# A gated recurrence and a long convolution on one core: h in time order with wrap copies, x1·x3 beside the spectral units, products summed by the inverse transform

## The chip, the cores and the metric

The kernel runs on one core of a Trainium2 chip. The core has a matrix engine (TensorE, PE in the profile, with its weight loads as PEld), a vector engine (VectorE, DVE), a scalar engine (ScalarE, ACT), a general engine (GpSimd, POOL), and a queue that here issues the transfers (SyncE, SP). Each works through its own list of instructions in order. The metric is device time in microseconds of one execution. All times below are microseconds unless ns is said.

## The reference

The inputs are x and f_logit of shape (4, 6272, 256): four batches (B), 6272 time steps (S), 256 channels (D). First comes a gated recurrence over time, then a projection into three parts, a circular convolution over the whole length by Fourier transform, a product of three, and an output projection:

```python
sig = 1.0 / (1.0 + np.exp(-f_logit))
f = lower_bound + (1.0 - lower_bound) * sig
for t in range(S):
    h = f[:, t] * h + (1.0 - f[:, t]) * x[:, t]
    y[:, t] = h
proj = y @ w_proj                          # 256 -> 3 x 256
x1, x2, x3 = proj[..., :D], proj[..., D:2*D], proj[..., 2*D:]
conv = irfft(rfft(x2, axis=1) * rfft(filter_fft, axis=0), n=S, axis=1)
out = (x1 * conv * x3) @ w_out
```

## The kernel before, in words

The transform of length 6272 is split into 128 × 49: with indices taken modulo S, a time step is addressed either as 49·m + r (natural order, m up to 128, r up to 49) or as 128·q + 49·m modulo S (rotated order, q up to 49). For each r there is one q (`Q_OF_R`), and the rows of one order are those of the other turned round by m0 (`m0_of`). So the transform is one of length 128 over m, followed by one of length 49 over q, with no twiddle factors between. `NEP` = 128 pairs of channels are worked in `NU` = 16 units of 8.

**hgrn(b)**, the recurrence, goes over 16 chunks of 392 time steps. Per chunk: x and f_logit are loaded (SP), the gate is a sigmoid on ACT, `xt` the product of x and gate on POOL (L123); 16 fp32 transposes on TensorE bring channels onto partitions (`sT`, `uT`); ACT makes `fT`, DVE runs the scan (L138), and POOL copies h out of natural order into `hG`, grouped by r (L143).

**prepare** builds the transform's matrices, the weights in high and low fp16 parts, and the filter's spectrum `H`: the filter is loaded in seven pieces (`fraw`), turned by 98 fp32 matmuls with a rotated identity (`pr`, L293), cast by ACT and DVE into `f2h` and `f2l` (L297, L298), and transformed in 16 units (`pfa`, `pfx`).

**phase_p(b)** copies h from `hG` into rotated order, `hP`, on POOL (L364, L366), multiplies by the x2 weights (`pp`) and evacuates on ACT (L370). **phase_f1(b)** does the 128-point transform, evacuated in turn by DVE (L386) and ACT (L388) into `A`. **phase_z(b)** computes x1·x3: eight 512-column matmuls with high and low weights (L406), x1 evacuated by ACT (`x1s`, L411), the product by DVE (L412). **mini(b)** does the frequency-0 column apart (`pm`, `zm`, L421). **units(b)**: per unit the 49-point transform (`px`, four matmuls, L442); the complex product with `H` as two wide multiplies (L446, L447) and two adds into `Y` (L450, L451) on DVE; POOL writes the frequency-0 column (L452); eight inverse matmuls (`pi`, L457, L459) with matrices `VA`, `VB`; ACT evacuates into `Th` (L463). **phase_o(b)**: the inverse over 128 (`pc`, L478), the product with x1·x3 on DVE (L482), the output projection (`po`, L491), ACT (L495), a store on SP.

The order is set in two ways. `weave` interleaves the loops of two phases by step count: recurrence of batch 0 with prepare; p, then f1, with x1·x3; units with the next batch's recurrence. Then a scheduler lists the instructions of each engine by that order as priority and by what is ready in its own reckoning, and the engines keep that list. PSUM tiles come from pools with one or two buffers: one for px (`psx`), two shared by all that is called `m` (`psm`), two for the transposes (`pst`).

## Time and profile before

| | |
|---|---|
| median of 3 runs | 1229.44 (1226.43 to 1230.41) |
| profiled execution | 1228.79, its span 1227.1 |
| mean granted TensorE clock | 0.803 of full speed |
| HBM | 58.85 MB read, 25.69 MB written |
| first x1·x3 matmul of batch 0, 1, 2, 3 | 242, 505, 765, 1015 |

The span runs from the first to the last instruction of the profiled execution. A busy share is an average over stages that have different limits, so the span is read stage by stage: preparation to 240, then four batches. The chain of waits is the work that ended last, followed back from the end; the timeline lists instructions by start. Matmuls overlap in the array, so four of them in a row take less than four times the length of one.

### The profile page before, as it was taken

To read this page: it belongs to the slowest core of one execution; us is meant where nothing else is said; L and a number is where in the kernel's file an instruction comes from. 1 tells how busy PE (TensorE), PEld (TensorE's weight loads), DVE (VectorE), ACT (ScalarE), POOL (GpSimd) and SP (SyncE) were. 2 spreads that over 40 slices of the span, in tenths; PEclk is the share of its full clock that TensorE was granted. 3 is DMA by queue.
4 is the path that set the end of the run, shared out by engine and by line. 5 is a ranking of instruction groups with operands and counts; after the bars stand their busy time and mean duration, and the time that the engine had idled before them with its cause. 6 is when DMAs were issued, how large, how long until landed. Compare 5 with 4: busy or idle time off the path is not lost.

```text
span 1227.1 us, 14846 instructions
## 1 busy us (share of the span) xinstructions
PE 892.4 (73%) x5784; PEld 577.3 (47%) x5784; DVE 639.7 (52%) x806; ACT 504.3 (41%) x649; POOL 386.8 (32%) x701
## 2 busy tenths in 40 slices
PE   2676789886678848776778677867788568767765
PEld 1444566443355536543455455434455454333344
DVE  7766743123579834223779632235898322346632
ACT  5676754463233324543333324633333226321122
POOL 5433441450136593000346761001465800000000
PEclk9996599999955569999755579998655799995579
DMA  6344411000023425100233334000233130000013
GB/s 199 97 124 122 122 56 51 28 1 1 2 78 105 114 78 190 65 1 1 53 82 111 97 123 168 1 1 26 68 106 91 52 141 19 1 1 0 1 69 142
DMA packets 61350, 85.50 MB, mean 70 GB/s; under 512 B 3040, under 2 KB 53984, under 8 KB 61280
## 3 DMA queue, kind: packets, MB, share of 16 engines
q1 hardware_dynamic: 61280, 84.55, 21.9%
q8 instruction: 45, 0.74, 0.3%
q14 instruction: 25, 0.20, 0.1%
HBM read 58.85 MB, written 25.69 MB: 69 GB/s over the span
## 4 chain that ended last, share of the span: by engine, by line
PE 46%; DVE 28%; POOL 9%; ACT 8%; issue 7%; DMA 3%; POOLq 0%; SPq 0%; DVEq 0%; ACTq 0%
PE p L406 15%; PE po L491 8%; PE px L442 5%; DVE z L482 4%; DVE p L446 4%; DVE z L412 4%; DVE Y L451 4%; ACT x1s L411 4%; PE pfx L324 3%; PE pr L293 3%; DVE A L386 3%; DVE h L138 3%; POOL hP L366 3%; POOL xt L123 3%; PE pc L478 2%
## 5 line engine op out<-in xcount | busy, mean ns | idle before, releaser
L143 POOL CAST hG<-h 128x392 f16<-128x392 f32 x128 | 109.6, 861 | 359.9 <-PE p L406 262.2
L406 PE MATMUL p<-hG,W13h 128*128 128x512 f16 (+1 forms) x416 | 150.3, 368 | 83.2 <-DVE z L412 42.5
L123 POOL TENSOR_TENSOR xt<-xt,ft 98x1024 f32<-98x1024 f32 x64 | 157.4, 2461 | 131.5 <-DMA xt<-in_x_dram 54.9
L412 DVE TENSOR_TENSOR z<-p,x1s 128x512 f16<-128x512 f32 (+1 forms) x104 | 68.4, 658 | 182.4 <-ACT x1s L411 182.4
L463 ACT CAST Th<-pi 128x784 f16<-128x784 f32 x64 | 52.0, 812 | 245.9 <-PE pi L459 245.9
L406 PE MATMUL p<-hG,W13l 128*128 128x512 f16 (+1 forms) x416 | 150.3, 367 | 0.0
L132 PE MATMUL uT<-iden,xt 98*128 98x98 f32 x512 | 107.2, 353 | 53.5 <-ACT fT L135 27.9
L482 DVE TENSOR_TENSOR z<-pc,z 128x1024 f16<-128x1024 f32 (+1 forms) x52 | 60.5, 1163 | 153.7 <-PE pc L478 153.7
L491 PE MATMUL po<-Woh,z 128*128 128x256 f16 x392 | 99.3, 294 | 55.1 <-DVE z L482 53.2
L442 PE MATMUL px<-A,FT 98*128 98x512 f16 x256 | 118.9, 593 | 27.0 <-DVE p L447 20.4
L411 ACT ACTIVATE x1s<-p 128x512 f32<-128x512 f32 (+1 forms) x104 | 59.5, 572 | 169.1 <-PE p L406 168.6
L138 DVE TENSOR_TENSOR_SCAN h<-fT,h,uT 128x392 f32<-128x392 f32 x120 | 120.6, 1024 | 11.2 <-PE uT L132 7.1
L132 PEld LDWEIGHTS uT<-iden,xt 98*128 98x128 f32 x512 | 80.0, 206 | 85.1 <-ACT fT L135 43.5
L128 PE MATMUL sT<-iden,ft 98*128 98x98 f32 x512 | 105.3, 352 | 19.4 <-ACT ft L122 16.0
L457 PE MATMUL pi<-VA,Y 98*128 98x196 f16 x256 | 84.4, 364 | 43.9 <-POOL Y L452 43.9
L491 PEld LDWEIGHTS <-z 128*128 128x128 f16 x784 | 77.9, 105 | 77.1 <-DVE z L482 62.2
L446 DVE TENSOR_TENSOR p<-px,H 98x1024 f16<-98x1024 f32 x64 | 78.2, 1222 | 64.0 <-PE px L442 64.0
L128 PEld LDWEIGHTS sT<-iden,ft 98*128 98x128 f32 x512 | 83.2, 210 | 45.2 <-issue 14.9
L495 ACT ACTIVATE osb<-po 128x1024 f32<-128x1024 f32 (+1 forms) x52 | 50.6, 974 | 129.0 <-PE po L491 122.4
L406 PEld LDWEIGHTS <-W13l 128*128 128x128 f16 x416 | 40.5, 97 | 131.5 <-issue 97.1
L135 ACT ACTIVATE fT<-sT,nomc 128x392 f32<-128x392 f32 x128 | 77.4, 605 | 53.7 <-PE sT L128 51.4
L491 PE MATMUL po<-Wol,z 128*128 128x256 f16 x392 | 98.6, 292 | 0.0
(129 smaller groups left out, 1522.4 us busy)
## 6 DMA issues: line engine op xcount, KB each, us to landing
xt<-in_x_dram SPq DMA_DIRECT2D x64, 392.0 KB
ft<-in_f_logit_dram SPq DMA_DIRECT2D x64, 392.0 KB
out_dram<-osb SPq DMA_DIRECT2D x48, 512.0 KB
fraw<-in_moe_filter_fft_dram SPq DMA_DIRECT2D x7, 896.0 KB
...
wcol<-in_lower_bound_dram SPq DMA_DIRECT2D x1, 1.0 KB
```

The costliest lines, as they stand in the source:

```text
L123: nc.gpsimd.tensor_tensor(xt[:TB], xt[:TB], ft[:TB], op=AOP.mult)
L128: nc.tensor.transpose(sT[:, j * TB:(j + 1) * TB], ft[:TB, j, cols], iden[:TB, :TB])
L132: nc.tensor.transpose(uT[:, j * TB:(j + 1) * TB], xt[:TB, j, cols], iden[:TB, :TB])
L138: nc.vector.tensor_tensor_scan(h32[:], fT[:], uT[:, 0:CH], 0.0 if last[kh] is None else last[kh][:, CH - 1:CH], op0=AOP.mult, op1=AOP.add)
L143: nc.gpsimd.tensor_copy(hG[b][:, kh, :, c * MR:(c + 1) * MR], h32[:].rearrange("p (m r) -> p r m", r=Q))
L406: nc.tensor.matmul(p13[:, i, 0:cn], w[:, kh, js], hG[b][:, kh, r0:r0 + rn, :], start=(n == 0), stop=(n == 3))
L411: nc.scalar.activation(x1s[:, 0:cn], p13[:, 0, 0:cn], AF.Copy, scale=ZS)
L412: nc.vector.tensor_tensor(z[:, jb, r0:r0 + rn, :], p13[:, 1, 0:cn], x1s[:, 0:cn], op=AOP.mult)
L442: nc.tensor.matmul(px[:, o, :], FT[:TB, tb, :], A[:TB, es, r, :], start=(n == 0), stop=(n == 1))
L446: nc.vector.tensor_tensor(p0[:TB], px[:TB], H[:TB, :, u, :], op=AOP.mult)
L482: nc.vector.tensor_tensor(zz, pc[:, :, 0:rn * 128].rearrange("p a (i m) -> p a i m", m=128), zz, op=AOP.mult)
L491: nc.tensor.matmul(po[:, i, :], z[:, kh, r0 + i, :], w[:, kh, :], start=(n == 0), stop=(n == 3))
```

## The change

Eight things are done together.

1. **h stays in time order.** The scan writes fp16 straight into one tile `HA`, which holds h of the first 128 channels (columns 0 to S), a middle part of 16384 columns, and h of the other 128 channels. Chunks are 512 steps on 128 partitions (13 chunks, the last of 128). `hG` and `hP` and their copies on POOL are gone.
2. **Wrap copies.** The rotated order needs h to go on after its end. Six SBUF-to-SBUF transfers a batch on SP's queue (`wraps`) put a copy of h beside itself, in the middle part. phase_p then reads its weights from `HA` with a column step of 49. The middle part is also where the forward transform `A` lies afterwards, and where the raw filter and weights are loaded at the start.
3. **x1·x3 moves** from beside phase_p and phase_f1 to beside the units and the next batch's recurrence: 13 groups of 490 time steps in natural order; its product is written into `z` by r, so it reads with a step of 49.
4. **No adds.** DVE's two multiplies take one half of the px bank pair each, against both halves of `H`, into `PP`; the inverse takes all four products, 16 matmuls with `VA`, `VB`, `VB` and `VN` = −`VA`, which add up in PSUM.
5. **POOL's frequency-0 copy** stands ahead of the products.
6. **PSUM is one tile** of eight banks. In the merged stage px has banks 0 and 1, pi 2 and 3, x1·x3 4 and 5, the transposes 6 and 7; elsewhere four bank pairs go round (`pair`).
7. **The filter is rotated by its loads**: for each q one or two transfers of 1 KB rows, 97 in all, in place of seven loads and 98 matmuls; ACT and DVE cast seven q at a time.
8. **The loops**: p and f1 run alone; units, x1·x3 and the next recurrence are stepped together; then wraps, output, and the next p and f1.

```diff
-CH = TB * NBLK
-NCHK = S // CH
+CH = 512
+NCHK = 13
+ZR = 10
+NZ = 13
+EW = NEP * 128
+E0 = S - 176
...
+    HA = konst.tile([128, 2 * S + EW], F16, name="HA")
+    A = HA[:, S:S + EW].rearrange("m (e r k) -> m e r k", r=2, k=64)
+    HB = (0, S + EW)
+    PP = konst.tile([128, 2, 2, 2, UE, 64], F16, name="PP")
...
+    PS = psp.tile([128, 8, 512], F32, name="PS")
+    turn = [0]
+    def pair():
+        turn[0] = (turn[0] + 1) % 4
+        return PS[:, 2 * turn[0]:2 * turn[0] + 2]
...
                 nc.vector.tensor_tensor_scan(
-                    h32[:], fT[:], uT[:, 0:CH],
-                    0.0 if last[kh] is None else last[kh][:, CH - 1:CH],
-                    op0=AOP.mult, op1=AOP.add)
-                last[kh] = h32
-                nc.gpsimd.tensor_copy(
-                    hG[b][:, kh, :, c * MR:(c + 1) * MR],
-                    h32[:].rearrange("p (m r) -> p r m", r=Q))
+                    HA[:, h0:h0 + n], fT[:, 0:n], uT,
+                    0.0 if c == 0 else HA[:, h0 - 1:h0], op0=AOP.mult, op1=AOP.add)
...
+    def wraps():
+        for a, z in ((0, 2048), (2048, 4096), (4096, E0)):
+            nc.sync.dma_start(HA[:, S + a:S + z], HA[:, a:z])
+        for a, z in ((128, 2048), (2048, 4096), (4096, S)):
+            nc.sync.dma_start(HA[:, HB[1] - S + a:HB[1] - S + z], HA[:, HB[1] + a:HB[1] + z])
...
-            raw = tmp.tile([128, 7, D], F32, name="fraw", tag="fraw", bufs=2)
-            nc.sync.dma_start(raw, ff[:, r0:r0 + 7, :])
...
+            for q in range(q0, q0 + 7):
+                mm = -((128 * q - S) // Q)
+                nc.sync.dma_start(raw[0:mm, q - q0, :],
+                                  moe_filter_fft[128 * q:128 * q + Q * (mm - 1) + 1:Q, :])
+                if mm < 128:
+                    s0 = 128 * q + Q * mm - S
+                    nc.sync.dma_start(raw[mm:128, q - q0, :],
+                                      moe_filter_fft[s0:s0 + Q * (127 - mm) + 1:Q, :])
...
-                nc.gpsimd.tensor_copy(hP[:, :, q, 0:128 - m0], hG[b][:, :, r, m0:128])
-                if m0:
-                    nc.gpsimd.tensor_copy(hP[:, :, q, 128 - m0:128], hG[b][:, :, r, 0:m0])
                 for kh in range(2):
-                    nc.tensor.matmul(pp[:, q - q0, :], hP[:, kh, q, :], W2[:, kh, :],
-                                     start=(kh == 0), stop=(kh == 1))
+                    n0 = HB[kh] + 128 * q - (S if kh and q else 0)
+                    nc.tensor.matmul(pp[:, q - q0, :], HA[:, n0:n0 + Q * 127 + 1:Q],
+                                     W2[:, kh, :], start=(kh == 0), stop=(kh == 1))
...
+                nc.vector.tensor_tensor(
+                    z[:, jb, :, m0:m0 + mn],
+                    PS[:, 5, 0:cn].rearrange("p (m r) -> p r m", r=Q),
+                    x1s[:, 0:cn].rearrange("p (m r) -> p r m", r=Q), op=AOP.mult)
...
-            nc.vector.tensor_tensor(p0[:TB], px[:TB], H[:TB, :, u, :], op=AOP.mult)
-            nc.vector.tensor_tensor(p1[:TB], px[:TB], H[:TB, ::-1, u, :], op=AOP.mult)
...
-            nc.vector.tensor_tensor(yf[:TB, 0], p0[:TB, 0], p0[:TB, 1], op=AOP.subtract)
-            nc.vector.tensor_tensor(yf[:TB, 1], p1[:TB, 0], p1[:TB, 1], op=AOP.add)
...
+                nc.vector.tensor_tensor(P[:TB, o, :, :, 1:64],
+                                        px.unsqueeze(1).broadcast_to([TB, 2, UE, 63]), hh,
+                                        op=AOP.mult)
...
+                for n, (a, h, v) in enumerate(((0, 0, VA), (0, 1, VB), (1, 0, VB),
+                                               (1, 1, VN))):
+                    nc.tensor.matmul(o, P[:TB, a, h, 2 * pr:2 * pr + 2, :], v[:TB],
+                                     start=(n == 0), stop=(n == 3))
...
+    wraps()
+    run(phase_p(0))
+    run(phase_f1(0))
     for b in range(B):
-        weave((seq(phase_p(b), phase_f1(b)), 13 + NU), (phase_z(b), 26))
         mini(b)
+        gu, gz = units(b), phase_z(b)
+        gh = hgrn(b + 1) if b + 1 < B else iter(())
+        for step in range(NU):
+            next(gz, None)
+            next(gu)
+            if step >= 2:
+                next(gh, None)
...
         if b + 1 < B:
-            weave((units(b), NU), (hgrn(b + 1), NCHK))
-        else:
-            run(units(b))
+            wraps()
         run(phase_o(b))
+        if b + 1 < B:
+            run(phase_p(b + 1))
+            run(phase_f1(b + 1))
```

Where instructions now stand is shown at three places. First DVE in the units with the recurrence. Before, one step of the loop (p products, Y adds, h scans):

```order
L446 TENSOR_TENSOR p_5286<-px,H 98x1024
L447 TENSOR_TENSOR p_5287<-px,H 98x1024
L450 TENSOR_TENSOR Y<-p_5286 98x512
L451 TENSOR_TENSOR Y<-p_5287 98x512
L138 SCALAR_TENSOR_TENSOR h_5322<-fT,h_5263,uT 128x392
L138 SCALAR_TENSOR_TENSOR h_5337<-fT,h_5278,uT 128x392
```

and with the change, two steps (PP products, scans into HA, z = x1·x3):

```order
L461 TENSOR_TENSOR PP<-PS,H 98x16x63 x2
L155 SCALAR_TENSOR_TENSOR HA<-fT,HA,PS 128x512 x2
L422 TENSOR_TENSOR z<-PS,x1s 128x49x10 x2
L461 TENSOR_TENSOR PP<-PS,H 98x16x63 x2
L155 SCALAR_TENSOR_TENSOR HA<-fT,HA,PS 128x512 x2
L422 TENSOR_TENSOR z<-PS,x1s 128x49x10 x2
```

The adds are gone, and two x1·x3 multiplies have come in behind the scans.

Second, TensorE at the same place. Before, the end of a unit's inverse (pi) and the transposes:

```order
L457 LDWEIGHTS Y
L457 MATMUL pi<-VA,Y 128x196
L459 LDWEIGHTS Y
L459 MATMUL pi<-VB,Y 128x196
L442 LDWEIGHTS FT
L442 MATMUL px<-A,FT 128x512
L128 MATMUL sT<-iden,ft 128x98 x4
L132 MATMUL uT<-iden,xt 128x98 x4
L128 MATMUL sT<-iden,ft 128x98 x4
L132 MATMUL uT<-iden,xt 128x98 x4
```

and now, from the last px matmul (L457) over the first transposes and one x1·x3 matmul (L416) to the first inverse matmuls (L469):

```order
L457 MATMUL PS<-HA,FT 128x512
L148 MATMUL PS<-iden,sr 128x128 x4
L150 MATMUL PS<-iden,ur 128x128 x4
L416 LDWEIGHTS W13h
L416 MATMUL PS<-HA,W13h 128x490
L469 LDWEIGHTS PP
L469 MATMUL PS<-VA,PP 128x196
L469 LDWEIGHTS PP
L469 MATMUL PS<-VB,PP 128x196
L469 LDWEIGHTS PP
L469 MATMUL PS<-VA,PP 128x196
```

A step on TensorE now reads: 4 px, 4 + 4 transposes, 1 of x1·x3, 4 inverse, 4 transposes, 2 of x1·x3, 12 inverse, 4 transposes, 13 of x1·x3.

Third, SP's queue at the start. Before, the filter came in whole pieces between the loads of x and f_logit:

```order
L257 DMA wp<-in_moe_w_proj_dram 128x2x768
L259 DMA wo<-in_moe_w_out_dram 128x2x256
L287 DMA fraw<-in_moe_filter_fft_dram 128x1792
L118 DMA xt<-in_x_dram 98x4x256
L120 DMA ft<-in_f_logit_dram 98x4x256
L287 DMA fraw<-in_moe_filter_fft_dram 128x1792
```

and now, after the same two weight loads:

```order
L308 DMA HA<-in_moe_filter_fft_dram 128x256
L308 DMA HA<-in_moe_filter_fft_dram 126x256
L312 DMA HA<-in_moe_filter_fft_dram 2x256
L308 DMA HA<-in_moe_filter_fft_dram 123x256
L312 DMA HA<-in_moe_filter_fft_dram 5x256
L308 DMA HA<-in_moe_filter_fft_dram 121x256
L312 DMA HA<-in_moe_filter_fft_dram 7x256
```

The second chunk of x stands behind 13 such loads, and the fifth behind all 97.

219 lines of the change are left out of this document (100 added, 119 removed).

## The prediction, on record before the result

> **What bounds the kernel now.** I read the page's totals and clock row first, then the stretches cut where the stages change, then the chain of waits and the timeline inside one stage. No engine is full over the whole span:
>
> ```profile
> PE 892.4 (73%) x5784; PEld 577.3 (47%) x5784; DVE 639.7 (52%) x806; ACT 504.3 (41%) x649; POOL 386.8 (32%) x701
> ```
>
> The stretches (start:end, length, busy time and count of PE, PEld, DVE, ACT, POOL, then clock, DMA share, GB/s) show stages with different limits:
>
> ```profile
> 0.00:240.00 240.00, 169.86 (x984) 115.15 (x984) 139.40 (x250) 147.85 (x205) 93.12 (x110) 0.89 0.35 102
> 505.00:591.00 86.00, 62.33 (x414) 34.85 (x414) 27.29 (x37) 37.93 (x45) 2.88 (x4) 1.00 0.00 1
> 591.00:691.00 100.00, 80.77 (x369) 54.34 (x367) 81.19 (x87) 35.07 (x49) 51.19 (x51) 0.54 0.34 94
> 691.00:721.00 30.00, 17.05 (x121) 12.43 (x119) 9.77 (x11) 7.23 (x9) 29.66 (x104) 0.56 0.21 73
> 721.00:765.00 44.00, 35.02 (x378) 26.66 (x377) 15.86 (x16) 18.61 (x22) 8.67 (x4) 0.95 0.52 178
> 851.00:950.00 99.00, 79.32 (x373) 53.44 (x371) 86.73 (x88) 35.29 (x49) 51.99 (x52) 0.56 0.32 90
> 1099.00:1173.00 74.00, 51.75 (x194) 26.05 (x192) 50.56 (x69) 12.18 (x15) 4.05 (x16) 0.51 0.00 0
> ```
>
> Batch 1 is the four rows from 505: x1·x3 with the forward transform (86 us, POOL idle), spectral units with the next batch's recurrence (100, DVE 81% busy, TensorE at half clock), the copies of h into rotated order (30, POOL 99% busy), output (44). The middle two show their bounds, the one in the timeline (start, length, engine, line, instruction), the other in the chain of waits (start, length, what), which then runs into the output:
>
> ```profile
> 373.29 1.21 DVE L447 TENSOR_TENSOR p<-px,H 98x1024 f16<-98x1024 f32 x1
> 374.42 0.41 DVE L450 TENSOR_TENSOR Y<-p 98x512 f16<-98x512 f16 x1
> 374.69 2.35 POOL L123 TENSOR_TENSOR xt<-xt,ft 98x1024 f32<-98x1024 f32 x1 [1.50 <-PE sT L128]
> 374.75 2.56 DVE L451 TENSOR_TENSOR Y<-p 98x512 f16<-98x512 f16 x1
> 377.24 1.94 DVE L138 TENSOR_TENSOR_SCAN h<-fT,h,uT 128x392 f32<-128x392 f32 x2
> ```
>
> ```profile
> 693.04 5.27 POOL hP L366 x27
> 705.07 10.53 POOL hP L364 x42
> 727.38 1.92 PE po L491 x16
> 731.18 1.92 PE po L491 x16
> ```
>
> Of the two like-sized adds on DVE, one takes 0.41 and the other, under POOL's multiply, 2.56. A recurrence step is 1.2 + 1.2 + 0.4 + 2.6 + 1.9 = 7.3 on DVE. In output a group of four rows takes 3.80.
>
> **The change part by part.** The sum is over stages, against the profiled execution (span 1227.1, time 1228.8; the median is 1229.4).
>
> Unit prices, first from the timeline:
>
> ```profile
> 243.27 0.64 PE L406 MATMUL p<-hG,W13h 128*128 128x512 f16 x1
> 243.70 0.63 PE L406 MATMUL p<-hG,W13l 128*128 128x512 f16 x1
> 244.67 0.38 PE L406 MATMUL p<-hG,W13h 128*128 128x512 f16 x1
> 244.89 0.38 PE L406 MATMUL p<-hG,W13l 128*128 128x512 f16 x1
> 181.81 0.50 PE L132 MATMUL uT<-iden,xt 98*128 98x98 f32 x4
> 381.44 0.92 PE L128 MATMUL sT<-iden,ft 98*128 98x98 f32 x4
> 480.64 0.62 PE L478 MATMUL pc<-ID,Th 64*128 64x128 f16 x16
> ```
>
> and from the groups by shape (line, engine, instruction, count, then busy in all and mean ns of one, then idle time before):
>
> ```profile
> L412 DVE TENSOR_TENSOR z<-p,x1s 128x512 f16<-128x512 f32 x96 | 66.1, 689 | 178.3 <-ACT x1s L411 178.3
> L138 DVE TENSOR_TENSOR_SCAN h<-fT,h,uT 128x392 f32<-128x392 f32 x120 | 120.6, 1024 | 11.2 <-PE uT L132 7.1
> L446 DVE TENSOR_TENSOR p<-px,H 98x1024 f16<-98x1024 f32 x64 | 78.2, 1222 | 64.0 <-PE px L442 64.0
> L370 ACT CAST x<-pp 128x1024 f16<-128x1024 f32 x48 | 67.8, 1412 | 14.3 <-PE pp L368 14.3
> L386 DVE CAST A<-pa 98x1024 f16<-98x1024 f32 x32 | 39.1, 1223 | 63.3 <-PE pa L382 63.3
> ```
>
> Start to start a 512-column matmul takes 0.43 at half clock and 0.22 at full: 490 columns are 0.207, 196 are 0.083. Four transposes of 128 columns come to about 0.5 at full clock, 1.1 at half. A scan of 512 instead of 392 is 1.3.
>
> *Merged stage (x1·x3, units, next recurrence).* Removed: both adds, the CASTs into hG, the wait of the inverse for POOL's copy, which now precedes the products. Added: 8 inverse matmuls a unit, and a wait that was not there: in TensorE's order the first four inverse matmuls stand ahead of transposes and x1·x3, so while they wait for P1 those wait too, and DVE's second scan waits for the transposes. By the order above, DVE does P0, P1, scan, scan, z, z, and TensorE stands in order before each. The loop that closes through DVE: P0 and P1 2.44; TensorE then has 4 inverse matmuls, 4 transposes, 2 of z, 12 inverse, 4 transposes: 0.33 + 0.5 + 0.41 + 1.0 + 0.5 = 2.74; second scan 1.3; z multiply 1.0; the last four x3 matmuls, whose PSUM bank waits for that multiply, 0.83; second z multiply 1.0; four handovers of 0.2 (a matmul's end outlasts its slot by 0.16). Together 10.1, while TensorE's own work is 7.5. All at half clock, TensorE alone is 14.3, with a wait 14.6.
>
> The z multiply now reads with a stride of 49 and writes runs of ten. Bounds: 0.69 (row above) and 2.2, by the row of DVE's strided access, 745 ns for 128 elements, or 4.6 ns each:
>
> ```profile
> L298 DVE TENSOR_TENSOR f2l<-pr,f2h 128x128 f16<-128x128 f32 x98 | 67.3, 745 | 26.8 <-ACT f2h L297 24.8
> L421 PE MATMUL pm<-A,FT 98*128 98x256 f16 x8 | 4.1, 598 | 0.0
> L335 PE MATMUL pfm<-mX,FT 98*128 98x256 f16 x4 | 0.7, 276 | 1.1 <-ACT H L327 1.1
> ```
>
> I take 1.0: that row writes single elements, the new one runs of ten. The clock: the rows at 243 to 244 show a dense run of x1·x3 lifting it from half to full within two microseconds, and the f1/x1·x3 stage stays at 1.00 with TensorE 72% busy. The new step has 16 such matmuls (at half clock 13 of them and the four of px stand in one block of 7 us), and a wait of some 2 us before the inverse. I charge a fifth of the time at half clock: 10.1 + 0.2 × 4.5 = 11.0. Steps 0 and 1 have no recurrence (7.5), steps 2 to 12 all three (11.0), 13 to 15 no z (13 together), the small transform 3: 15 + 121 + 13 + 3 = **152** for batches 0 to 2, in place of 86 + 100 less the forward transform. Batch 3, without scans and transposes: 13 × 7.8 + 13 + 3 = **117**.
>
> *Forward (p, f1), now alone.* POOL's 98 copies leave. ACT's 13 copies are 13 × 1.41 = 18.3. The weights are now read from h with a stride of 49. A strided moving operand took 598 against 276, 1.26 ns a column; on 128 columns of weights that would be 0.16 more than the 0.1 of a plain load, 98 × 0.26 = 25. Bounds 18 and 26, taken 22, between them. f1: 8 DVE copies of 1.22 and as many on ACT beside them, 10, and 1 to fill: **33**. Hiding is gone here: x1·x3 no longer covers ACT.
>
> *Output.* Two pc groups, then two po groups. Pair: pc 0.6, handover 0.2, multiply 1.2, then 2 × 1.75 for po = 5.5, where two groups took 7.6; six pairs, a last group, 2 for the cold start: **39**. The wrap copies, six of half a MB per batch, are DMA work in place of POOL's; four of them are left when the last unit is done. Output covers them: at its 178 GB/s they would take 12 a batch if nothing did. The next batch's x loads stand behind them on SP, but are two chunks ahead of their use.
>
> *Prologue.* Seven filter loads of 7 KB rows become 97 of 1 KB rows, and x loads stand behind them on SP's queue. What a transfer with an uneven number of rows uses is in the packet count:
>
> ```profile
> DMA packets 61350, 85.50 MB, mean 70 GB/s; under 512 B 3040, under 2 KB 53984, under 8 KB 61280
> ```
>
> 3040 small packets are 256 for wcol, 16 completions for each of 62 full transfers (52 out, 7 fraw, wp, wo, wcol) and 14 for each of the 128 with 98 rows: 256 + 992 + 1792. So 98 rows go on 14 engines, seven each. With even shares, 20 of the 97 loads (prime counts over 16) would run on one engine; summed over all, if the same engine is always the first, it gets 2,172 of 6,272 rows. A 1 KB packet costs 16 × 0.32 × 1024 / 90 = 58 ns (row of 851): 126, plus 64 rows for each of four recurrence chunks ahead, 15. Spread over all engines, the filter would take 23, less than 97 issues. Bounds for the filter's arrival 50 and 145; I take 130, near the one that the count supports. The Trainium skill (DMA: Bandwidth & Descriptors, section on why a DMA increments its semaphore by 16) states this rule: the largest divisor up to 16, always the lowest-numbered engines; the 14 above agree, and by it the arrival would be the 145. Then 5 for the last casts, 83 for the 16 units (157 to 240 now), 7 for the last wraps: **225** against 242 (145 to 240).
>
> Sum: 225 + 3 × (33 + 152 + 39) + 33 + 117 + 45 with the last store = 1092, and 2 outside the span: **1094**.
>
> **The rivals.** *Half clock in the merged stage (ends slower).* For it: units run at 0.51 to 0.56 now with TensorE called 70 to 80% busy, and a quarter of the new step is transposes. Against it: the rows at 243. Price: 14.6 for 11.0 on 11 steps and three batches, 119, and 3 on 13 steps of batch 3, 39: 1252. It decides from about 14 a step, that is nearly all steps cold. The Trainium skill (TensorE: Matmul & The Clock Gate, Part 4) says that transposes do not count as busy for the gate; no row here separates that, and it would make this rival likelier.
>
> *Strides dear.* z multiply 2.2 and p 26: 1.2 × 2 on each of 52 steps, 125, and 4 × 4: 1235. For it the 4.6 ns; against it the runs of ten.
>
> *Filter spread on all engines.* Prologue 145: 1014. Against it the 14 engines.
>
> *More hidden than I count*: full clock throughout, z multiply 0.7 (two on each of 52 steps): less 38 and 31, 1025. For it the dense run's quick lift; against it the 2 us wait in each step.
>
> That the copies reappear elsewhere, so that nothing is gained, I exclude: the 30 us of POOL per batch has no successor on any engine but DMA.
>
> **How the numbers follow.** My sum 0.52, half clock 0.12, strides 0.12, filter spread 0.10, more hidden 0.14. The likeliest case's own range is 1050 to 1150. For eight in ten, 1000 to 1238: either gaining rival on one side, dear strides on the other; half clock lies outside. This kernel is measured to about 0.3%, so same means 1225 to 1233. Half clock and the upper part of dear strides are slower, 0.15; some of dear strides is the same, 0.03; the rest, 0.82, is faster.
>
> **What would show it.** Right: POOL under a fifth of the span; no stretch with POOL alone; recurrence steps of 10 to 12 us with TensorE waiting for P1 before the inverse; p near 22 us; filter loads landing until about 130. Wrong: a clock row near 0.5 in the merged stretches (first rival), z multiplies above 1.5 us (second), the f2h casts done by 60 us (third), steps under 9.5 (fourth). If p or output is longer than before, a cover that I took as free has a price.

## The result and the profile after

The changed kernel takes 932.89 us (median of 4, 931.39 to 934.82), the kernel before 1228.89 beside it: a ratio of 0.759 (0.757 to 0.762). The forecast was 1094, with a range from 1000 to 1238. The direction was right; the gain of 296 is more than twice the forecast 135.

Totals on the page of the changed kernel, and its stretches cut where the stages change (start:end, length, busy time and count of PE, PEld, DVE, ACT, POOL, then clock, DMA share, GB/s):

```profile
PE 716.7 (77%) x5958; PEld 499.3 (54%) x5958; DVE 533.9 (57%) x585; ACT 434.7 (47%) x541; POOL 145.4 (16%) x173
```

```profile
0.00:120.00 120.00, 17.04 (x64) 11.87 (x64) 55.56 (x134) 41.97 (x51) 16.17 (x28) 1.00 0.37 113
120.00:218.00 98.00, 86.92 (x713) 57.17 (x713) 43.27 (x38) 54.06 (x66) 28.67 (x43) 1.00 0.41 129
218.00:240.00 22.00, 13.87 (x101) 11.90 (x102) 0.50 (x2) 18.76 (x21) 2.34 (x1) 0.85 0.22 74
250.00:369.00 119.00, 107.13 (x726) 68.16 (x724) 92.72 (x89) 54.66 (x82) 32.98 (x29) 1.00 0.39 124
369.00:407.00 38.00, 32.53 (x415) 27.64 (x416) 14.59 (x14) 14.22 (x15) 0.00 (x0) 0.96 0.52 200
407.00:423.00 16.00, 9.92 (x82) 8.78 (x80) 0.00 (x0) 15.59 (x14) 0.00 (x0) 0.94 0.04 14
801.00:891.00 90.00, 82.10 (x526) 45.67 (x524) 62.73 (x62) 26.62 (x42) 3.94 (x16) 1.00 0.00 1
```

The first three are preparation and batch 0's p, the next three batch 0's merged stage and output and batch 1's p, the last batch 3's merged stage. Batch 1 took 260 before (the four rows from 505 in the prediction; its first x1·x3 matmul starts at 501.8, and those of batches 2 and 3 at 761.8 and 1012.2, some 3 earlier than the table at the front has them) and takes 183 now: p and f1 27, merged 119, output 37. POOL is nowhere busy alone, and the merged stage has a clock of 1.00.

DVE inside that stage, one step and the beginning of the next (start, length, instruction, and in brackets the idle time before it and who ended it):

```profile
301.70 2.30 DVE L461 TENSOR_TENSOR PP<-PS,H 98x1008 f16<-98x1008 f32 x2
303.93 1.26 DVE L155 TENSOR_TENSOR_SCAN HA<-fT,HA,PS 128x512 f16<-128x512 f32 x1
306.01 1.28 DVE L155 TENSOR_TENSOR_SCAN HA<-fT,HA,PS 128x512 f16<-128x512 f32 x1 [0.82 <-PE PS L150]
307.21 0.97 DVE L422 TENSOR_TENSOR z<-PS,x1s 128x490 f16<-128x490 f32 x1
309.32 1.00 DVE L422 TENSOR_TENSOR z<-PS,x1s 128x490 f16<-128x490 f32 x1 [1.15 <-PE PS L416]
310.24 1.20 DVE L461 TENSOR_TENSOR PP<-PS,H 98x1008 f16<-98x1008 f32 x1
```

and four rows of TensorE in the same step: the first inverse matmul, the first of the 12 that wait for P1, the uT transposes, and the x3 matmuls that wait for the first z multiply:

```profile
302.95 0.26 PE L469 MATMUL PS<-VA,PP 98*128 98x196 f16 x1 [0.33 <-DVE PP L461]
...
304.15 0.25 PE L469 MATMUL PS<-VB,PP 98*128 98x196 f16 x1
...
305.25 0.66 PE L150 MATMUL PS<-iden,ur 128*128 128x128 f32 x4
...
308.23 0.37 PE L416 MATMUL PS<-HA,W13h 128*128 128x490 f16 x1 [0.44 <-DVE z L422]
```

A step is 8.54 (301.70 to 310.24), and it closes on DVE: six operations and two gaps, 0.82 for the uT transposes and 1.15 for the last x3 matmuls. The first inverse matmul starts at 302.95, a full microsecond before P1, the second of the two products, is done (304.0).

### The profile page after: what moved, and what is told of

Its sections match the earlier page's. It is cut to its first block, busy times and chain, and to the rows that moved or that the text cites. A ratio compares the mean times of both kernels' runs of the same rounds, so it can differ in the third digit from the quotient of the medians.

```text
span 929.8 us, 14546 instructions
## 1 busy us (share of the span) xinstructions
PE 716.7 (77%) x5958; PEld 499.3 (54%) x5958; DVE 533.9 (57%) x585; ACT 434.7 (47%) x541; POOL 145.4 (16%) x173
## 4 chain that ended last, share of the span: by engine, by line
PE 39%; DVE 26%; issue 13%; ACT 9%; DMA 7%; SPq 3%; POOL 2%; DVEq 0%; ACTq 0%; POOLq 0%
PE PS L469 9%; PE PS L416 9%; PE PS L501 7%; DVE z L422 7%; DVE PP L461 7%; DMA HA<-in_moe_filter_fft_dram 6%; ACT x L382 5%; DVE HA L155 5%; PE PS L345 3%; PE PS L150 3%; DVE z L493 2%; PE PS L148 2%; PE PS L392 2%; POOL ur L142 2%; SPq L312 1%
## 5 line engine op out<-in xcount | busy, mean ns | idle before, releaser
L416 PE MATMUL PS<-HA,W13h 128*128 128x490 f16 (+1 forms) x416 | 152.3, 366 | 15.0 <-DVE z L422 14.8
L416 PE MATMUL PS<-HA,W13l 128*128 128x490 f16 (+1 forms) x416 | 152.3, 366 | 0.0
L155 DVE TENSOR_TENSOR_SCAN HA<-fT,HA,PS 128x512 f16<-128x512 f32 (+1 forms) x96 | 116.1, 1209 | 62.3 <-PE PS L150 42.9
L461 DVE TENSOR_TENSOR PP<-PS,H 98x1008 f16<-98x1008 f32 x128 | 149.1, 1197 | 1.7 <-PE PS L457 1.7
L422 DVE TENSOR_TENSOR z<-PS,x1s 128x490 f16<-128x490 f32 (+1 forms) x104 | 101.0, 971 | 69.5 <-PE PS L416 58.5
L142 POOL TENSOR_TENSOR ur<-xt,sr 128x1024 f32<-128x1024 f32 (+1 forms) x52 | 116.7, 2245 | 132.3 <-ACT sr L140 111.6
L469 PEld LDWEIGHTS <-PP 98*128 98x128 f16 x1024 | 82.8, 97 | 65.9 <-DVE PP L461 39.6
L501 PE MATMUL PS<-Woh,z 128*128 128x256 f16 x392 | 89.9, 278 | 20.8 <-DVE z L493 20.8
L469 PE MATMUL PS<-VB,PP 98*128 98x196 f16 x512 | 95.6, 248 | 4.6 <-DVE PP L461 4.5
L501 PE MATMUL PS<-Wol,z 128*128 128x256 f16 x392 | 89.5, 277 | 0.0
L469 PE MATMUL PS<-VA,PP 98*128 98x196 f16 x256 | 58.7, 248 | 19.9 <-DVE PP L461 17.1
```

Source lines behind the costliest of these rows:

```text
L142: nc.gpsimd.tensor_tensor(ur[:, 0:nb], xt[:, 0:nb], sr[:, 0:nb], op=AOP.mult)
L155: nc.vector.tensor_tensor_scan(HA[:, h0:h0 + n], fT[:, 0:n], uT, 0.0 if c == 0 else HA[:, h0 - 1:h0], op0=AOP.mult, op1=AOP.add)
L416: nc.tensor.matmul(PS[:, 4 + i, 0:cn], w[:, kh, js], HA[:, h0:h0 + cn], start=(n == 0), stop=(n == 3))
L422: nc.vector.tensor_tensor(z[:, jb, :, m0:m0 + mn], PS[:, 5, 0:cn].rearrange("p (m r) -> p r m", r=Q), x1s[:, 0:cn].rearrange("p (m r) -> p ...
L461: nc.vector.tensor_tensor(P[:TB, o, :, :, 1:64], px.unsqueeze(1).broadcast_to([TB, 2, UE, 63]), hh, op=AOP.mult)
L469: nc.tensor.matmul(o, P[:TB, a, h, 2 * pr:2 * pr + 2, :], v[:TB], start=(n == 0), stop=(n == 3))
```

## The experiments

Each is one profiled execution beside the kernel before on the same chip, where nothing else is said. Stage times are between the last evacuations by ACT of neighbouring stages.

### The wait for P1

```diff
-for n, (a, h, v) in enumerate(((0, 0, VA), (0, 1, VB), (1, 0, VB), (1, 1, VN))):
+for n, (a, h, v) in enumerate(((1, 0, VB), (1, 1, VN), (0, 0, VA), (0, 1, VB))):
```

> Edit: each group of the inverse begins with the two products of P1, so that all 16 inverse matmuls of a unit have to wait for P1, as the prediction wrongly had it for the first four. The work is the same. Theory A (the step closes through DVE; what stood ahead of the inverse in TensorE's order did not wait for P1, and what comes after P1 lies beside the first scan): 16 inverse matmuls of 0.083 behind P1 end about 0.3 later than now, the second scan starts 0.2 to 0.3 later, steps of 8.7 to 8.9, 938 to 948 in all. Theory B (the prediction's loop: transposes and x1*x3 caught behind that wait, 2.74 of TensorE between P1 and the second scan): steps of 10, that is 1.5 on each of 39 steps, 990. If the place of this wait does not matter at all: 933.

Measured: 925.1, eight less than the changed kernel and below all three expectations. In its timeline a step is 8.66:

```profile
301.88 2.31 DVE L461 TENSOR_TENSOR PP<-PS,H 98x1008 f16<-98x1008 f32 x2
...
306.32 1.28 DVE L155 TENSOR_TENSOR_SCAN HA<-fT,HA,PS 128x512 f16<-128x512 f32 x1 [0.94 <-PE PS L150]
...
310.54 2.33 DVE L461 TENSOR_TENSOR PP<-PS,H 98x1008 f16<-98x1008 f32 x2
```

All 16 inverse matmuls now wait for P1, and the gap before the second scan is 0.12 longer. The stages are shorter all the same (the merged stage 118 in place of 119, one output 36.9 in place of 39.4); the order of TensorE's list changed with the edit, and what of it gains this is not shown. The loop of the prediction (10.1) is refuted: what comes after P1 lies under the first scan, whether the inverse starts early or not.

### x1·x3 apart, and the adds back

```diff
-        gu, gz = units(b), phase_z(b)
+        run(phase_z(b))
+        gu, gz = units(b), iter(())
```

> Edit: x1*x3 of a batch runs alone ahead of the units, which are then beside the next recurrence only. Both theories pay for what is no longer beside other work: x1*x3 alone 45 to 60 a batch. Theory A (the clock in the units is held at full by the dense x1*x3 matmuls): without them the stretch of units and recurrence falls to a granted clock near 0.5, as in the kernel before, with steps near 9: 1150 to 1200. Theory B (the clock is full because TensorE no longer waits for adds and copies, whatever runs beside): the stretch stays above 0.9, steps near 6: 1030 to 1060.

Measured: 962.7, less than either theory. The merged stage with x1·x3 ahead of it is 124 to 128 a batch, against 119; batch 3 has 101 for 91. x1·x3 alone takes 55 to 58, units with recurrence 66 to 71, at a clock of 1.00. So that x1·x3 stands beside the units is worth 30 us of the 296, and it does not hold the clock.

```diff
+            nc.vector.tensor_tensor(P[:TB, 0, 0], P[:TB, 0, 0], P[:TB, 1, 1], op=AOP.subtract)
+            nc.vector.tensor_tensor(P[:TB, 0, 1], P[:TB, 0, 1], P[:TB, 1, 0], op=AOP.add)
-                for n, (a, h, v) in enumerate(((0, 0, VA), (0, 1, VB), (1, 0, VB), (1, 1, VN))):
+                for n, (a, v) in enumerate(((0, VA), (1, VB))):
```

> Edit: DVE adds the products again (in place, two operations of 98x512 in fp16 a unit), and the inverse takes 8 matmuls in place of 16. All else as in the changed kernel. Theory A (an add costs DVE 0.41 unless POOL's multiply runs at the same time, and that one now runs under the second scan): 0.8 more on DVE's loop in a step, 9.3 to 9.5, 970 to 980 in all. Theory B (the adds cost what they cost before, 0.41 and 2.56): 3 more a step, 1060. Theory C (TensorE is what sets the step, so 8 matmuls fewer win): 900 to 930.

Measured: 917.8, 15 faster than without adds. Its DVE timeline:

```profile
299.19 1.21 DVE L461 TENSOR_TENSOR PP<-PS,H 98x1008 f16<-98x1008 f32 x1
...
302.47 1.28 DVE L155 TENSOR_TENSOR_SCAN HA<-fT,HA,PS 128x512 f16<-128x512 f32 x1
303.66 0.41 DVE L464 TENSOR_TENSOR PP<-PP 98x512 f16<-98x512 f16 x1
303.98 0.42 DVE L465 TENSOR_TENSOR PP<-PP 98x512 f16<-98x512 f16 x1
305.35 1.28 DVE L155 TENSOR_TENSOR_SCAN HA<-fT,HA,PS 128x512 f16<-128x512 f32 x1 [0.95 <-PE PS L150]
```

The adds cost 0.41 each, and they do not fill the gap before the second scan: it is still 0.95, and from scan to scan it is 2.88 where it was 2.08. The time comes back elsewhere. A product (299.19) now stands between the two z multiplies, where DVE waited 1.15, and a step is 8.23 (first scan to first scan, 302.47 to 310.70); in batch 1 it is 7.69, with one gap of 0.44. The total lies where theory C (8 matmuls fewer win) had it, but the order of the lists changed with the edit, and the two are not told apart. So this part of the change (four products summed in PSUM) costs time here. The groups of the kernel before say what the adds cost there:

```profile
L451 DVE TENSOR_TENSOR Y<-p 98x512 f16<-98x512 f16 x64 | 67.6, 1056 | 0.0
L450 DVE TENSOR_TENSOR Y<-p 98x512 f16<-98x512 f16 x64 | 34.3, 535 | 0.0
```

1.6 a unit on average, not the 3.0 of the step that the prediction quoted; that step is one of those in which the second add fell under POOL's multiply.

### What lifted the clock

The same two edits together:

> Edit: in the changed kernel x1*x3 of a batch runs alone ahead of the units, and DVE adds the products again (8 inverse matmuls). So beside the recurrence TensorE has 3.6 of work a step and DVE 5.7, much as in the kernel before. Theory A (the granted clock follows how densely TensorE is fed: in the kernel before it was near 0.5 because TensorE waited for DVE, whatever else changed): the stretch of units and recurrence falls below 0.8, its steps go from 4.3 to 6 or 7, and the time is 20 to 40 a batch above the kernel with x1*x3 alone apart (963): 1020 to 1090. Theory B (the full clock comes from the other parts of the change: no copies of h, scans into fp16, PSUM as one tile): the clock stays at 0.95 or more, the step is DVE's 5.7 to 6, 980 to 1040.

Measured: 985.9; units with recurrence 70 to 76, units alone in batch 3 50. The stretches of batch 0 and batch 3:

```profile
314.00:380.00 66.00, 48.95 (x327) 30.92 (x326) 63.77 (x76) 35.07 (x49) 30.40 (x24) 0.97 0.77 240
893.00:944.00 51.00, 40.85 (x170) 22.10 (x170) 42.06 (x57) 12.16 (x15) 3.31 (x13) 0.58 0.00 0
```

The first row is theory B's. Yet the second, batch 3's units, shows half clock, and with 16 inverse matmuls in place of 8 (the run with x1·x3 apart) they have 1.00:

```profile
880.00:922.00 42.00, 35.87 (x287) 23.78 (x284) 31.96 (x28) 11.78 (x15) 3.29 (x13) 1.00 0.00 1
```

TensorE with the adds back, first in units alone, then beside the recurrence:

```profile
898.63 0.59 PE L457 MATMUL PS<-HA,FT 98*128 98x512 f16 x2 [0.43 <-DVE PP L461]
901.53 2.13 PE L457 MATMUL PS<-HA,FT 98*128 98x512 f16 x4 [0.43 <-DVE PP L461]
...
325.23 0.63 PE L150 MATMUL PS<-iden,ur 128*128 128x128 f32 x4 [0.69 <-DVE HA L155]
325.69 0.60 PE L148 MATMUL PS<-iden,sr 128*128 128x128 f32 x4
330.47 0.63 PE L150 MATMUL PS<-iden,ur 128*128 128x128 f32 x4 [0.69 <-DVE HA L155]
```

Alone, a unit takes 2.9 (898.63 to 901.53) and holds, start to start, 0.87 of px and 0.66 of inverse, 53%: the clock falls at 901. Beside the recurrence a step takes 5.24 (325.23 to 330.47) and holds the same 1.53 and four times 0.46 of transposes, 64%: the clock stays. The Trainium skill (TensorE: Matmul & The Clock Gate, Part 4) says that transposes do not count as busy in the same way for the gate. By that rule the step with 29% other work would be the first to fall; this trace disagrees, for these fp32 transposes, which the profile lists as matmuls by `iden`. The share alone does not give a rule either: from 919 on, at half clock, a unit takes 3.62 and holds 1.72 of px and 1.31 of inverse, 84%, and the clock does not come back.

In the kernel before, TensorE was made busier without use: eight matmuls of 120 columns behind each four transposes.

```diff
+                if b:
+                    for t in (sT, uT):
+                        for k in range(8):
+                            nc.tensor.matmul(t[:, 392:512], D1[:], D1[:, 0:120],
+                                             start=True, stop=True)
```

> Edit, in the kernel before: behind each four transposes of the recurrences of batch 1 to 3, TensorE does eight more matmuls of 120 columns whose results nobody reads (32 a step, 1.8 at full clock). Theory A (the granted clock follows how much of the time TensorE is fed, and at half clock the stretch is bound by TensorE): more work lifts the clock in the stretch of units and recurrence above 0.8, and it falls from 113 to 85 to 105, 1130 to 1200 in all. Theory B (the clock does not answer to that, or the stretch is DVE's): 1228 to 1330.

Measured: 1223.4, beside 1229.4. Units with recurrence in batch 1, first of the kernel before, then of this one:

```profile
591.00:704.00 113.00, 87.67 (x404) 59.68 (x401) 87.29 (x94) 38.73 (x55) 63.85 (x99) 0.54 0.33 93
```

```profile
590.00:700.00 110.00, 81.10 (x801) 64.21 (x800) 88.79 (x93) 38.74 (x53) 61.92 (x94) 0.89 0.32 92
```

The clock rises from 0.54 to 0.89, as theory A has it, and the stage goes from 116.1 to 115.2, which it has not. So the half clock there goes with a loosely fed TensorE: more matmuls lift it. Whether it also set the time, this run does not show, since the fillers cost time of their own: they write the banks that the scans read, and the scans wait for them. Their idle time before grew from 11.2 (the prediction's row of L138) to 83.3, and 68.4 of it ended with a filler (L137):

```profile
L143 DVE TENSOR_TENSOR_SCAN h<-fT,h,uT 128x392 f32<-128x392 f32 x120 | 123.8, 1032 | 83.3 <-PE uT L137 68.4 <-ACT fT L140 5.1 <-PE uT L132 5.0
```

What the clock alone was worth stays open. The next runs ask what shortened the loop.

### What shortened units with recurrence

First parts of the change made alone in the kernel before. No adds:

```diff
-            nc.vector.tensor_tensor(yf[:TB, 0], p0[:TB, 0], p0[:TB, 1], op=AOP.subtract)
-            nc.vector.tensor_tensor(yf[:TB, 1], p1[:TB, 0], p1[:TB, 1], op=AOP.add)
-            nc.gpsimd.tensor_copy(Y[:TB, :, :, 0], zm[:TB, :, es])
+            nc.gpsimd.tensor_copy(v0[:TB, 0, :, 0], zm[:TB, 0, es])
+            nc.gpsimd.tensor_copy(v1[:TB, 0, :, 0], zm[:TB, 1, es])
...
+                for n, (v, r, w) in enumerate(((v0, 0, VA), (v0, 1, VN), (v1, 0, VB), (v1, 1, VB))):
```

> Edit, in the kernel before: only one part of the change is made, the products are accumulated by 16 inverse matmuls and the two adds on DVE are gone. Layout, recurrence, copies on POOL and x1*x3 stay as before. Theory A (the clock in units with recurrence was low because TensorE stood waiting for DVE's 7.3 a step; with 4.4 on DVE, TensorE with 4.7 of its own work at full clock is dense and the clock rises by itself): the stretch of 100 falls to 70 to 80 at a clock above 0.8, the last one of 74 to 50 to 60; 1130 to 1160 in all. Theory B (the clock stays at half whatever DVE does): 8 more matmuls of 0.166 and transposes at half clock make TensorE the bound with 9 or more a step, the stretch is 100 to 120, 1200 to 1290 in all.

Measured: 1248.3, 18 slower than before. Units with recurrence fall from between 114 and 116 a batch to between 104 and 110, at a clock of 0.73 to 0.86, but batch 3's units grow from 75 to 110. The first inverse matmuls wait for POOL (line, engine, instruction, count, busy, mean ns, idle before):

```profile
L461 PE MATMUL pi<-VA,p 98*128 98x196 f16 x256 | 80.4, 314 | 67.1 <-POOL p L454 66.6
```

With POOL's copies ahead of the products:

```diff
+            for v, c, h in ((v0, 0, hk), (v1, 1, hk[:, ::-1])):
+                nc.gpsimd.tensor_copy(v[:TB, 0, :, 0], zm[:TB, c, es])
+                nc.gpsimd.memset(v[:TB, 1, :, 0], 0.0)
+                nc.vector.tensor_tensor(v[:TB, :, :, 1:64], xk, h, op=AOP.mult)
```

> Edit, in the kernel before: the products are accumulated by 16 inverse matmuls, without adds, as in the earlier run, and POOL's frequency-0 copies now stand ahead of the products, so that the inverse waits for DVE alone. Theory A (in the earlier run the gain of the adds was taken by POOL's copies, which stood behind the products and in POOL's queue behind its multiply and its copies of h; 67 us of waiting there): the stretch of units and recurrence falls from 104 to 110 to 75 to 90, the last one, without recurrence, from 110 to 55 to 75, 1110 to 1160 in all. Theory B (POOL's copy is not what holds it, but px's single PSUM buffer or the transposes): 1230 to 1250.

Measured: 1208.2; 93 to 96 a batch, and batch 3 still 110 at half clock, so POOL was not what held it there. And POOL's copy ahead with the adds kept:

```diff
+            nc.gpsimd.tensor_copy(Y[:TB, :, :, 0], zm[:TB, :, es])
-            nc.vector.tensor_tensor(yf[:TB, 0], p0[:TB, 0], p0[:TB, 1], op=AOP.subtract)
-            nc.vector.tensor_tensor(yf[:TB, 1], p1[:TB, 0], p1[:TB, 1], op=AOP.add)
-            nc.gpsimd.tensor_copy(Y[:TB, :, :, 0], zm[:TB, :, es])
...
+            nc.vector.tensor_tensor(Y[:TB, 0, :, 1:64], k0[:, 0], k0[:, 1], op=AOP.subtract)
+            nc.vector.tensor_tensor(Y[:TB, 1, :, 1:64], k1[:, 0], k1[:, 1], op=AOP.add)
```

> Edit, in the kernel before: POOL writes the frequency-0 column of Y ahead of the adds, which leave it out; the adds stay. Theory A (TensorE stood thin in units with recurrence because each inverse waited for POOL, whose queue holds the gate multiply and the copies of h): the clock there rises from 0.54 to 0.8 or more, the stretch falls from 113 to 85 to 95, 1130 to 1170 in all. Theory B (that wait is 44 of all and hidden elsewhere; the low clock has another cause): 1210 to 1235, clock below 0.65.

Measured: 1215.9; 100 to 102 a batch, clock 0.63 to 0.69, batch 3 94. Between its two theories: 14 a batch are gained, 43 in all, and 19 of them lost again in batch 3 and 13 in longer outputs. A row of batch 3 shows what holds it, and a row of the run with x1·x3 apart and the adds back, in its batch 3, what does there:

```profile
1105.27 1.03 PE L442 MATMUL px<-A,FT 98*128 98x512 f16 x2 [2.45 <-DVE p L447]
```

```profile
924.35 1.01 PE L457 MATMUL PS<-HA,FT 98*128 98x512 f16 x2 [0.44 <-DVE PP L461]
```

The two multiplies of this kernel both read the whole of px, so the next px stands until the second is done, 2.45 in a unit of 5.64. In the changed kernel each multiply reads one bank, and the next px into the first bank can start when the first multiply is done. With as many matmuls, the same products and adds, POOL's copy ahead and the clock at half for the most part (0.58), batch 3's units take 51 there, a unit 3.62 with a wait of 0.44. That this is the reason is argued: no run undoes this part alone.

Then the other way, parts undone one after another in the changed kernel, beginning with x1·x3 apart and the adds back (985.9). POOL behind the adds:

```diff
-            nc.gpsimd.tensor_copy(P[:TB, 0, :, :, 0], zm[:TB, :, es])
...
             nc.vector.tensor_tensor(P[:TB, 0, 1], P[:TB, 0, 1], P[:TB, 1, 0], op=AOP.add)
+            nc.gpsimd.tensor_copy(P[:TB, 0, :, :, 0], zm[:TB, :, es])
```

> Edit, to the kernel with x1*x3 apart and the adds back (985.9, clock 0.97 in units with recurrence): POOL writes the frequency-0 column behind the adds, as in the kernel before, so the inverse waits for POOL. Theory A (this wait is what thinned TensorE before): the stretch of 66 grows to 75 to 95 and its clock falls below 0.8, 1010 to 1070 in all. Theory B (POOL has only the gate multiply left in its queue and comes in time): 983 to 1000.

Measured: 999.8, theory B's. And POOL copies h to nowhere:

```diff
+                if b:
+                    hs = cw.tile([128, CH], F32, name="hs", tag="x1s")
+                    nc.gpsimd.tensor_copy(hs[:, 0:n], HA[:, h0:h0 + n])
```

> Edit: as the last, and POOL also copies each scan's h into a spare tile that nobody reads (two copies of 128x512 a step), in place of the copies into rotated layout that the kernel before had there. Theory A (POOL's queue, with copies that wait for DVE's scans ahead of the frequency-0 column, is what thinned TensorE in the kernel before): 10 to 30 a batch above the last kernel, 1020 to 1090, with a clock below 0.8 in units. Theory B (POOL's load does not matter here): within 10 of the last.

Measured: 1016.1, 16 above the last, between its theories; the clock stays above 0.9, and the add beside POOL's copy takes 0.82 for 0.42. And the old chunks:

```diff
-CH = 512
-NCHK = 13
+CH = 392
+NCHK = 16
...
-            if step >= 2:
-                next(gh, None)
+            next(gh, None)
```

> Edit: to the kernel with x1*x3 apart, adds back, POOL behind the adds and POOL's spare copies (1016.1), the recurrence goes again in 16 chunks of 392 steps on 98 partitions, one in each of the 16 steps, in place of 13 of 512. Then the stretch of units and recurrence has all that it had in the kernel before, but for the layout of h. Theory A (a step has a fixed cost in waits between TensorE, ACT and DVE, so 16 chunks cost more than 13, and this makes most of what still separates the 77 of the last kernel from the 113 before): the stretch grows to 90 to 110 a batch, 1055 to 1115 in all. Theory B (chunk size does not matter): 1005 to 1030, and the rest of the difference has another cause.

Measured: 1111.1 (16 of the rise are in the preparation, which has the same chunks). Units with recurrence, from the last z multiply to the last evacuation of the inverse, mean of batches 0 to 2:

| kernel | us a batch |
|---|---|
| changed, x1·x3 apart | 69 |
| and adds on DVE | 72 |
| and POOL's copy behind the adds | 75 |
| and POOL copies h | 80 |
| and 16 chunks of 392 | 107 |
| kernel before | 115 |

The largest part, 26 of 46, is one whose gain the prediction does not name, though its sum counts the new steps: 13 chunks in place of 16. DVE in the last two kernels of the ladder, 13 chunks, then 16:

```profile
547.65 0.39 DVE L466 TENSOR_TENSOR PP<-PP 98x512 f16<-98x512 f16 x1
...
548.71 1.19 DVE L463 TENSOR_TENSOR PP<-PS,H 98x1008 f16<-98x1008 f32 x1
549.83 1.27 DVE L155 TENSOR_TENSOR_SCAN HA<-fT,HA,PS 128x512 f16<-128x512 f32 x1
551.01 1.18 DVE L463 TENSOR_TENSOR PP<-PS,H 98x1008 f16<-98x1008 f32 x1
552.11 1.26 DVE L155 TENSOR_TENSOR_SCAN HA<-fT,HA,PS 128x512 f16<-128x512 f32 x1
553.30 0.39 DVE L466 TENSOR_TENSOR PP<-PP 98x512 f16<-98x512 f16 x1
```

```profile
565.64 2.30 DVE L462 TENSOR_TENSOR PP<-PS,H 98x1008 f16<-98x1008 f32 x2
569.08 1.03 DVE L154 TENSOR_TENSOR_SCAN HA<-fT,HA,PS 128x392 f16<-128x392 f32 x1 [1.14 <-PE PS L149]
...
572.42 1.03 DVE L154 TENSOR_TENSOR_SCAN HA<-fT,HA,PS 128x392 f16<-128x392 f32 x1 [1.35 <-PE PS L149]
573.37 2.29 DVE L462 TENSOR_TENSOR PP<-PS,H 98x1008 f16<-98x1008 f32 x2
```

With 13 chunks DVE is listed product, scan, product, scan, and has no gap: 5.65 a step. With 16 the scheduler lists both products and then the scans, each of which waits over a microsecond here for transposes: 7.73 a step, and three steps more. The clock differs as well, 0.91 and 0.64 in the same stage of batch 1 (13 chunks, then 16):

```profile
509.00:590.00 81.00, 56.94 (x364) 37.59 (x364) 74.60 (x83) 38.90 (x53) 47.06 (x54) 0.91 0.61 198
```

```profile
552.00:665.00 113.00, 81.44 (x423) 58.44 (x421) 79.19 (x91) 44.46 (x61) 52.86 (x61) 0.64 0.43 130
```

In the step with 16 chunks shown, inverse matmuls start 0.16 apart, at half clock, and the transposes that the scans wait for are as slow. The run changed all three, so how much of the 26 is the count, how much the order that comes with it and how much the clock stays open; so does the last 8 to the kernel before, which still differs in the layout of h, the PSUM tiles and the multiplies that read the whole of px.

### The filter loads, p, and the z multiply

```diff
+                if mm < 128:
+                    mm = min(max(mm // 16 * 16, 16), 112)
```

> Edit: the 97 filter loads are kept, but each has a multiple of 16 rows (some rows of the filter are then wrong; bytes and issues are the same). Theory A (a load uses only as many DMA engines as divide its rows evenly, so odd row counts pile up on few engines): the last filter load lands at 45 to 70 in place of 113, the units begin 45 to 55 earlier, 880 to 890 in all. Theory B (the arrival is set by the number of issues on SP's queue, by buffers or by the casts): within 10 of now, 923 to 935.

Measured: 888.0, as theory A has it (some rows of the filter are then not the right ones). On SP's queue the last filter load is issued at 60.57 (111.6 in the changed kernel), and loads take 0.42 each, one behind the other:

```profile
60.10 0.42 SPq L311 DMA_DIRECT2D HA<-in_moe_filter_fft_dram  x1
60.57 0.42 SPq L315 DMA_DIRECT2D HA<-in_moe_filter_fft_dram  x1
```

So uneven row counts, not the number of loads, held the filter back, and cost 45.

```diff
+                for k0, n, s0 in ((0, mm, 128 * q), (mm, 128 - mm, 128 * q + Q * mm - S)):
+                    for a, z in ((0, n // 16 * 16), (n // 16 * 16, n)):
+                        if z > a:
+                            sa = s0 + Q * a
+                            nc.sync.dma_start(raw[k0 + a:k0 + z, q - q0, :],
+                                              moe_filter_fft[sa:sa + Q * (z - a - 1) + 1:Q, :])
```

> Edit: each filter load is split into a part with a multiple of 16 rows and a remainder of at most 15; all rows are right, there are nearly twice as many loads (about 190). Theory A (even shares on the engines set the arrival): the first engine's rows fall to about a sixteenth, issues of 0.3 each now take some 60, the last filter load lands at 60 to 75, 890 to 905 in all. Theory B (the run with multiples of 16 gained by something else, and the number of issues sets the arrival): as late as now or later, 930 to 950.

Measured: 905.7. 176 loads, the last at 86.5: now the issues are the bound.

```diff
-            nc.scalar.copy(xv[:, :, q0:q0 + qn],
-                           pp[:, 0:qn, :].rearrange("m q e -> m e q"))
+            cp = nc.scalar.copy if q0 // 4 % 2 else nc.vector.tensor_copy
+            cp(xv[:, :, q0:q0 + qn], pp[:, 0:qn, :].rearrange("m q e -> m e q"))
```

> Edit: the 13 copies that empty x2's PSUM banks in p are made by DVE and ACT in turn, in place of ACT alone. Theory A (p is ACT's 13 copies of 1.50; the weight loads with a column step of 49 are not on the path): p falls by 6 to 9 a batch, 900 to 910 in all. Theory B (the strided weight loads on TensorE set p): no change, 930 to 936.

Measured: 902.3; from the end of output to the end of p 10.2, for 15.3, and p with f1 falls from 26.9 to 20.1 in batch 1, near theory A's 6 to 9. Three groups of the changed kernel show why (ACT's copies; the weight loads with a column step of 49, where plain ones took 98; the z multiply):

```profile
L382 ACT CAST x<-PS 128x1024 f16<-128x1024 f32 x48 | 62.4, 1498 | 4.9 <-PE PS L380 4.9
L380 PEld LDWEIGHTS <-HA 128*128 128x128 f16 x392 | 44.6, 144 | 12.9 <-issue 8.2 <-DMA HA<-HA 2.9 <-DVE HA L155 0.2
L422 DVE TENSOR_TENSOR z<-PS,x1s 128x490 f16<-128x490 f32 x96 | 94.5, 985 | 64.8 <-PE PS L416 55.6 <-ACT x1s L421 4.1 <-ACT Th L472 2.3
```

```diff
-                    z[:, jb, :, m0:m0 + mn],
-                    PS[:, 5, 0:cn].rearrange("p (m r) -> p r m", r=Q),
-                    x1s[:, 0:cn].rearrange("p (m r) -> p r m", r=Q), op=AOP.mult)
+                    z[:, jb].rearrange("p r m -> p (r m)")[:, m0 * Q:m0 * Q + cn],
+                    PS[:, 5, 0:cn], x1s[:, 0:cn], op=AOP.mult)
```

> Edit, in the changed kernel: the z multiply reads and writes in natural order, without the step of 49 (so output later takes the products in a wrong order). Theory A (the multiply is on DVE's loop twice a step): it falls from 0.985 to 0.7, the step from 8.55 to 8.0, batch 3's too by 0.3 to 0.6: 900 to 915 in all. Theory B (the step has slack there): 928 to 935.

Measured: 900.5, as theory A has it (z is then in an order that the output does not read); the multiply takes 0.64 to 0.67 and a step 7.88. So the stride costs 0.33 each, in full on the path: 32 in all.

### A version that beats both

```diff
                     0.0 if c == 0 else HA[:, h0 - 1:h0], op0=AOP.mult, op1=AOP.add)
-            yield
+                if b or kh:
+                    yield
...
                     x1s[:, 0:cn].rearrange("p (m r) -> p r m", r=Q), op=AOP.mult)
-            yield
+                yield
...
-            next(gz, None)
             next(gu)
-            if step >= 2:
-                next(gh, None)
+            for kh in range(2):
+                next(gz, None)
+                if step >= 2:
+                    next(gh, None)
```

> Edit: within a step of the changed kernel the work is listed in the order unit, first half of x1*x3, first half of the recurrence, second half of x1*x3, second half of the recurrence, so DVE has P0, P1, z, scan, z, scan. The work is the same. Theory A (a step is DVE's 6.8 of work and two idle gaps of 0.82 and 1.15, which come from two scans and two z multiplies standing back to back on one PSUM bank each): the gaps are covered, and the step falls from 8.55 to TensorE's own 7.5 to 7.9; 26 to 41 less on 39 steps, 890 to 907 in all. Theory B (the step is set by something else, TensorE's order or ACT): within 10 of now, 923 to 943.

Measured: 917.1. A step is 8.02; the merged stage falls from 119 to 113. In a step TensorE now has one gap, 0.53, and DVE two, 0.37 and 0.89: theory A in direction, with 16 of its 26 to 41.

The three gains together, with loads of seven q at a time where no q wraps within the rows:

```diff
+            lo, hi = min(mq) // 16 * 16, min(128, -(-max(mq) // 16) * 16)
+            for m0, m1, s0 in ((0, lo, 128 * q0), (hi, 128, 128 * q0 + Q * hi - S)):
+                if m1 > m0:
+                    nc.sync.dma_start(raw[m0:m1], bass.AP(
+                        tensor=moe_filter_fft.tensor, offset=s0 * D,
+                        ap=[[Q * D, m1 - m0], [128 * D, 7], [1, D]]))
...
```

> Three edits of the changed kernel together: the alternated step; p emptied by DVE and ACT in turn; and filter loads of seven q at a time where none of them wraps within the rows (a multiple of 16 rows), with small loads for the rows in between, 109 loads in all. If they add up: 16 for the step, 30 for p, 40 to 45 for the loads: 840 to 850 in all. If the preparation has another bound below: 850 to 870.

Measured, median of 4: 848.4, a ratio to the kernel before of 0.690 (0.688 to 0.692). With the adds on DVE besides:

> The same three edits, and DVE adds the products again with 8 inverse matmuls. Theory A (TensorE, with 7.5 of work, sets the alternated step, so 8 matmuls fewer shorten it to about 7.7, DVE's own): 4 to 15 less than without adds. Theory B (the added 0.8 on DVE makes DVE the bound): 5 to 20 more than without adds.

Measured: 839.5, 0.683 (0.681 to 0.685). So the four-product inverse costs 9 here too, within theory A's 4 to 15; DVE is then 100 of 107 busy in the merged stage:

```profile
210.00:317.00 107.00, 91.98 (x588) 57.06 (x588) 100.29 (x118) 55.54 (x80) 33.17 (x29) 0.97 0.46 146
```

## Why the prediction was wrong, by its own steps

**The step of the merged stage (10.1) failed: its term of 2.74 for TensorE between P1 and the second scan.** It charged the first four inverse matmuls with a wait for P1. They are VA, VB, VA, VB, the two products of the first px bank (a = 0 in the loop), and need P0 alone; the names in the order that the front part shows say so, VN and the second VB being those of P1. So 4 inverse matmuls, 4 transposes and 2 of x1·x3 ran under P1. Nor was the rest a chain: the 12 others (1.0) ran beside the first scan (1.26), for which the uT transposes wait anyway, since the scan reads their bank. Start to start in the timeline above, with the prediction's terms and their handovers in brackets: products 2.23 (2.44), first to second scan 2.08 (2.74 and two handovers, 3.14), second scan 1.20 (1.3), z and the x3 matmuls 2.11 (2.23), second z 0.92 (1.0): 8.54 (10.1). The largest part of the difference, 1.06, is the term between the scans. That the inverse's start hardly matters, the first experiment shows: 0.12 a step.

**The 0.9 for half clock did not come**; the stage has 1.00. (Its 14.3 for TensorE alone at half clock, in the first rival, is 15.4 by its own prices.) The two errors make 2.45 a step. Ten full steps (25 a batch), and an eleventh that runs in with the end, make the 33 by which 152 was too much; three batches, 99. In batch 3 the step was 6.0 in place of 7.8 by the same waits: 27. This is the fourth rival's side (steps under 9.5), whose 1025 kept the wrong loop.

**The adds.** The prediction took 3.0 a step from one timeline row; the mean was 1.6. That number was in no term of the sum, which was built from the new loop, but it gave the wrong reason for the gain: with POOL out of the way the adds cost 0.8 a step, the run with them back wins more than that elsewhere in the step, and leaving them out makes the kernel slower by 15.

**Prologue 225, measured 218**: right by two errors. The last casts of the filter end at 122, not 135; the bound that the packet count supported (even shares) was right as a mechanism, and its size a little large. The 16 units then took 98, not 83: two of them and a recurrence chunk take 11.3. With the loads evened the gain was 45, not the 80 between 225 and the third rival's 145, since the casts then hold until 75 and the units still take 98.

**p and f1 33, measured 26 to 27** in batches 1 to 3. p is bound by ACT's 13 copies, not by weight loads. They are 1.50 long but start 1.28 apart (12 in 15.4), so that even the lower bound of 18 was too high, and one of them runs under the output's end. The strided weight load is 0.144, nearer the plain 0.098 than the bound of 0.26, and off the path. **Output 39, measured 38**; the last 39 in place of 45.

**The rivals.** Half clock and dear strides are refuted by the rows above. That the copies reappear nowhere was right: POOL is at 16%. The wrap copies are hidden but for 3 ahead of the first p, where TensorE waits 2.7 for the last of them.

**The signs named in advance**: POOL and the missing stretch of POOL held; steps of 10 to 12 with TensorE waiting for P1, p near 22 and loads until 130 did not.
